# Moving a one-row sum to another engine and giving a batch the cheaper channel product, in a Fourier mixing kernel on one core

## The chip, the cores and the metric

The kernel runs on one core of a Trainium2 chip. A core has five engines with a queue each: TensorE (PE; its weight loads are listed as PEld), VectorE (DVE), ScalarE (ACT), GpSimd (POOL) and SyncE (SP), the last of which here only issues DMAs. The engines run side by side, each takes its instructions in order, and they wait for one another through semaphores. The metric is the device time of one execution in microseconds. Before the change it is 447.11 us, the median of three runs (446.85 to 447.27).

## The reference

```python
# x: [8, 3136, 256]   U: [3136, 32]   V: [32, 3136]   w_ch1: [256, 1024]   w_ch2: [1024, 256]
X = np.fft.fft(x, axis=1)                  # along the sequence
X = np.fft.fft(X, axis=2)                  # along the channels
x = X.real
xt = x.transpose(0, 2, 1)
h = xt @ U @ V                             # low-rank mixing along the sequence, rank 32
u = x + h.transpose(0, 2, 1)
ch = np.maximum(u @ w_ch1, 0.0) @ w_ch2    # two-layer product per token
out = u + ch
```

The real part of the two transforms is a product with cosines on both sides minus a product with sines on both sides.

## The kernel before, in words

**Stages.** The eight batches of 3136 rows are one list of 25088 output rows, worked in 49 chunks of 512 (`CH`). For a chunk `c` the main loop runs eight steps `j`. In each, `first_product(c, j)` multiplies the chunk's `u` with an eighth of `w_ch1` (two matmuls of 512 columns, L735) and ScalarE applies the relu on the way out of PSUM (L737). At every odd `j`, `second_product(c - 1, j // 2)` makes 128 rows of the chunk before (eight matmuls of 256 columns, L751); each second time VectorE adds `u` to it (L757 to L760) and so frees one of two PSUM buffers. At `j == 3`, `front(c + 1)` makes the next chunk's `u`: `low_product` (L709) multiplies the low-rank factors `TA` and `VA`, and VectorE adds the transformed input `S` or `T` to both halves (L725).

**A batch's transform** runs ahead of the chunks that need it, in steps hung between those of the main loop. `fold(b)` loads the batch in halves and takes sums and differences of mirrored channels (`along_d`, L386), of mirrored rows (`mirror`, L395) and of the two halves (`half`, L399), all on VectorE, into `G`. It also issues the next batch's loads on GpSimd's queue. `seq(b, par, typ, pn)` is the transform along the sequence on TensorE: `typ` 1 is the cosine (result `A`), 0 the sine (result `B`), `par` the parity of the output index, `pn` the parity of the input tile. The even tiles (`pn == 0`) are multiplied first and ScalarE keeps the result in `ev` (L489); after the odd tiles VectorE writes their sum into one half of `A` or `B` (L500) and their difference into the other (L504). A group of 425 columns holds 393 of the transform and 32 (`QW - NQ`) that carry `U` along, from which `TF`, and by `join_t` (L468) `TAB`, arise. `halves` (L430) and `quarters` (L446) are cheaper forms of an even group: matmuls over about half of the columns, from which VectorE makes the other half with a sum and a difference (L436, L437). Before, batches from `B0 = 2` on use `quarters`; the second batch (`b == 1`) uses `halves` for the cosine alone; the first batch uses neither.

**The channel product** turns `A` and `B` into `S` and `T`. In the batches from `B0` on, `even_ch` (one matmul from `A`, L643; ScalarE keeps it, L645) and `odd_ch` (one matmul from `B`, L652) give `S` and `T` as their sum and difference on VectorE (L654), and `across` copies rows of `A` into the lower 64 rows of `VA` on ScalarE (L664, L666). The first two batches use `chan` instead: for each of four pieces and each half one matmul from `A` and one from `B` into the same PSUM buffer (L631, L633), which ScalarE copies out (L635); and `last_row` (L684) fills a row of `VA` on VectorE.

**The narrow part.** The channel with index 0 has a column of its own in `G`. `narrow` transforms it in 16 matmuls with a stationary operand 32 wide (L556); the result has one used row, at PSUM partitions 0, 32, 64 and 96 for the four combinations of parities. Six sums of one row follow: two of 32 elements (L570), two upward ones (L573) and two downward ones (L574). They go into `TF` and into row 32 (`R`) of `VA`, which `low_product` reads. For the first batch VectorE makes them straight from PSUM, and the downward ones later (`late`); for the second, GpSimd makes them from SBUF, after ScalarE has copied both halves out. For the six batches from `B0` on, one joint narrow part (`column_steps`) does it for all at once.

**What sets the order.** Up to the end of chunk 0's steps the order is the program's own (`manual_schedule`). From chunk 1 on a planner places the instructions, and those of `fold` keep their program order (`pin`). The steps between the main loop's are entered in `due` under the number 8 * c + j, by `spread(steps, lo, hi)`, which distributes a list evenly. Tiles of the setup phase lie in the pool `gen`, which is closed before the pool `cp` opens in the same space; the first tile of `cp` is `u0`, the first chunk's `u`, written in two halves at L977.

## Time and profile before

| | |
|---|---|
| Median of three runs | 447.11 us (446.85 to 447.27) |
| The profiled execution's own time | 447.31 us |
| Its span in the profile | 445.2 us |
| Granted TensorE clock | 1.00 of full speed |
| TensorE busy | 435.7 us, 98% |
| VectorE busy | 353.1 us, 79% |
| ScalarE busy | 297.5 us, 67% |
| GpSimd busy | 85.7 us, 19% |

A row of a timeline gives the start and the duration in microseconds, the engine, the line, the operation, the tiles (out <- in), partitions and elements, and how many such instructions were merged. In brackets stands idle time before it and what ended that. The durations of matmuls overlap, since the array is a pipeline: the distance from one start to the next is what a matmul takes of TensorE's time. A row of a group gives the count, the busy time and the mean of one in ns. A row of windows gives, for a stretch, the busy time and count of PE, PEld, DVE, ACT and POOL, then the granted clock, the DMA share and GB/s.

### The profile page before, as it was taken

What the parts mean: (1) busy time and instruction counts of PE and PEld (TensorE: products, weight loads), DVE (VectorE), ACT (ScalarE), POOL (GpSimd) and SP (SyncE); (2) the same over time, 40 slices, a digit from 0 to 9 for tenths busy, and PEclk for the clock granted to TensorE, in tenths of its full rate; (3) what the DMA queues carried; (4) which work ended last, traced back from release to release, by engine and by line L of the source; (5) the groups of instructions that cost most, each with busy time, mean ns of one, the idle gap of its engine ahead of it and who ended that gap; (6) DMA issues with size and microseconds to landing.
All of it is one profiled execution on the core that took longest, in us unless ns stands there. A gap on an engine that the chain in (4) does not pass through costs nothing.

```text
span 445.2 us, 8087 instructions
## 1 busy us (share of the span) xinstructions
PE 435.7 (98%) x2960; PEld 316.4 (71%) x3012; DVE 353.1 (79%) x838; ACT 297.5 (67%) x564; POOL 85.7 (19%) x144
## 2 busy tenths in 40 slices
PE   8999999999999999999999999999999999999997
PEld 6456766776677777777777777777777777777775
DVE  8879998888998799878998789878998776443433
ACT  8857747565885669655875569655876569656562
POOL 8973217300931002300211001300000000000000
PEclk9999999999999999999999999999999999999999
DMA  7998997995199437674779537782333332434343
GB/s 133 210 230 180 229 173 117 245 153 103 49 230 265 120 106 216 190 171 73 157 203 222 108 103 216 196 167 71 95 119 95 91 100 73 117 97 121 93 125 112
DMA packets 103249, 65.36 MB, mean 147 GB/s; under 512 B 73806, under 2 KB 99624, under 8 KB 100464
## 3 DMA queue, kind: packets, MB, share of 16 engines
q1 hardware_dynamic: 97528, 39.10, 40.1%
q0 software_dynamic: 5664, 25.75, 21.6%
q8 instruction: 23, 0.38, 0.3%
q14 instruction: 16, 0.13, 0.1%
q10 hardware_dynamic: 18, 0.00, 0.0%
HBM read 29.33 MB, written 25.69 MB: 124 GB/s over the span
## 4 chain that ended last, share of the span: by engine, by line
PE 91%; DVE 2%; DMA 2%; issue 1%; POOL 1%; ACT 1%; DVEq 0%; POOLq 0%
PE p L751 38%; PE p L735 35%; PE pt L485 6%; PE ph L709 5%; DMA xb<-in_x_dram,xidx 2%; PE ptq L446 2%; PE pst L643 1%; PE pst L652 1%; PE m L850 1%; PE ptc L556 1%; ACT h L737 0%; DVE eor L386 0%; PE pst L631 0%; DVE eof L386 0%; PE pst L633 0%
## 5 line engine op out<-in xcount | busy, mean ns | idle before, releaser
L737 ACT ACTIVATE h<-p 128x512 bf16<-128x512 f32 x392 | 222.0, 597 | 119.5 <-PE p L735 107.3
L735 PE MATMUL p<-u,w 128*128 128x512 bf16 x735 | 209.3, 379 | 1.2 <-DVE B L500 0.2
L751 PE MATMUL p<-w,h 128*128 128x256 bf16 x1568 | 203.0, 273 | 1.4
L751 PEld LDWEIGHTS <-h 128*128 128x128 bf16 x1568 | 153.2, 98 | 50.4 <-DVE o L760 0.3
L735 PEld LDWEIGHTS <-w 128*128 128x128 bf16 x784 | 106.1, 144 | 35.1 <-issue 2.0
L757 DVE TENSOR_TENSOR o<-p,ut 128x4 f32<-128x4 f32 (+1 forms) x100 | 16.2, 162 | 54.9 <-PE p L751 53.3
L759 DVE TENSOR_TENSOR o<-p,ut 128x254 f32<-128x254 f32 (+1 forms) x100 | 40.5, 405 | 0.0
L760 DVE TENSOR_TENSOR o<-p,ut 128x254 f32<-128x254 f32 (+1 forms) x100 | 40.5, 405 | 0.0
L468 POOL TENSOR_TENSOR tab<-tf 128x64 bf16<-128x64 f32 x7 | 3.1, 440 | 179.2 <-DVE tf L492 179.1
L386 DVE TENSOR_TENSOR eof<-xf 99x1024 bf16<-99x1024 f32 x28 | 35.8, 1293 | 0.0
L386 DVE TENSOR_TENSOR eor<-xr 99x1024 bf16<-99x1024 f32 x28 | 34.8, 1247 | 0.0
L725 DVE TENSOR_TENSOR u<-ph,S 128x512 bf16<-128x512 f32 (+23 forms) x63 | 34.3, 553 | 0.0
L725 DVE TENSOR_TENSOR u<-ph,T 128x512 bf16<-128x512 f32 (+23 forms) x63 | 34.2, 553 | 0.0
L55 POOL DMA_INDIRECT xf<-in_x_dram,xidx x14 | 17.3, 1234 | 62.0 <-DVE eof L386 48.5
L709 PE MATMUL ph<-va,ta 128*128 128x512 bf16 (+15 forms) x124 | 28.6, 328 | 0.3
L485 PEld LDWEIGHTS <-g 98*128 98x128 bf16 (+1 forms) x152 | 14.7, 98 | 13.1 <-issue 0.7
L395 DVE TENSOR_TENSOR eos<-eof,eor 99x1024 bf16<-99x1024 bf16 (+1 forms) x28 | 19.2, 702 | 0.0
L654 DVE TENSOR_TENSOR S<-evd,pst 128x392 bf16<-128x392 f32 (+1 forms) x24 | 13.5, 564 | 6.4 <-PE pst L652 4.1
L485 PE MATMUL pt<-tabs,g 98*128 98x425 bf16 x80 | 17.6, 344 | 0.0
L457 DVE TENSOR_TENSOR ev<-ptq,ex 128x131 f32<-128x131 f32 (+1 forms) x24 | 6.9, 289 | 12.9 <-ACT ex L450 12.9
L399 DVE TENSOR_TENSOR g<-eos 99x2048 bf16<-99x2048 bf16 (+1 forms) x14 | 16.9, 1217 | 0.0
L485 PE MATMUL pt<-tabc,g 98*128 98x425 bf16 x72 | 15.5, 344 | 0.0
(198 smaller groups left out, 381.0 us busy)
## 6 DMA issues: line engine op xcount, KB each, us to landing
out_dram<-o SPq DMA_DIRECT2D x48, 512.0 KB
xr<-in_x_dram POOLq DMA_DIRECT2D x14, 784.0 KB, 8.2
xb<-in_x_dram POOLq DMA_DIRECT2D x2, 392.0 KB, 7.9
ut<-u SPq DMA_TRANSPOSE x49
w<-in_moe_w_ch_dram POOLq DMA_DIRECT2D x1, 512.0 KB
out_dram<-o SPq DMA_DIRECT2D x4, 128.0 KB
va<-in_moe_V_dram POOLq DMA_DIRECT2D x2, 196.0 KB
w<-in_moe_w_ch_dram POOLq DMA_DIRECT2D x1, 256.0 KB, 7.2
```

The costliest lines, as they stand in the source:

```text
L55: nc.gpsimd.indirect_dma_start(out_, None, bass.AP(t.tensor, t.offset, [[w, rows], [1, w]]), bass.IndirectOffsetOnAxis(idx, 0), element_of ...
L386: pin(nc.vector.tensor_tensor(dst[:, a, :, part * P:(part + 1) * P].rearrange("p i (k t) -> p i k t", k=2), lo, hi, op=AL.subtract if part ...
L395: pin(nc.vector.tensor_tensor(EOS[:, a, :, cols], EOF_[:, a, :, cols], EOR_[:, a, ::-1][:, :, cols], op=op))
L399: pin(nc.vector.tensor_tensor(G[b % 2][par][:, :, cols], EOS[:, 0, :, cols], EOS[:, 1, :, cols], op=AL.add if par == 0 else AL.subtract))
L485: nc.tensor.matmul(pt[:], g[:kp(i), i, P * typ:P * (typ + 1)], tabs[typ][:kp(i), i, par, :], start=(n == 0), stop=(n == NI // 2 - 1))
L709: nc.tensor.matmul(ph, TA[b % 2][:k, s * P:(s + 1) * P], VA[b % 2][:k, lo:hi], start=start, stop=True)
L725: nc.vector.tensor_tensor(u[:, s, col:col + hi - lo], ph[:, col:col + hi - lo], src, op=AL.add)
L735: nc.tensor.matmul(p1[:], W1[:, s, j::JT], k["u"][:, s, :], start=(s == 0), stop=(s == 1))
L737: LAST[0] = nc.scalar.activation(k["h"][:, j, :], p1[:], AF.Relu)
L751: nc.tensor.matmul(p2[:, t % w, :], h[:, j, rs], W2[:, j, :], start=(j == 0), stop=(j == JT - 1))
L759: nc.vector.tensor_tensor(o[:, ts, 1:P], p2[:, :w, 1:P], ut[:, ts, 1:P], op=AL.add)
L760: nc.vector.tensor_tensor(o[:, ts, P + 1:D], p2[:, :w, P + 1:D], ut[:, tT, P - 1:0:-1], op=AL.add)
```

## The change

- **First batch, narrow part** (`single=True`): ScalarE copies the four used rows out of PSUM one by one, to partition 0 of two tiles in the pool `gen` (`parted`: two before the sums of the first parity, two in front of those of the second). GpSimd makes all six sums from them, the downward ones right behind the others. VectorE makes none. The tiles use the buffers of `pho`, which become wider.
- **Second batch, order**: its narrow part comes first in `transform`, ahead of the sequence transform. Its sums of 32 elements go to tiles of their own (`tc1`, `tr1`), which `joined` copies into `TAB`.
- **Second batch, sine**: its even sine groups use `halves` too.
- **Second batch, channels**: `even_ch`, `odd_ch` and `across` replace `chan`, `low_product` takes all 128 rows of `TA` and `VA`, and `last_row` is no longer called for it; fewer rows of its `VA` are zeroed.
- **Places in the order**: the second batch's fold and transform start two places earlier (2 and 21 instead of 4 and 23); the third batch's fold begins four places later and ends two later, its transform begins two later and ends where it did; six of the seven steps of the joint narrow part come two to three places later, and the last one a place earlier.

```diff
-        if pn == 0 and (b >= B0 or b == 1 and typ == 1):
+        if pn == 0 and b:
             (quarters if b >= B0 else halves)(d, g, par, typ)
...
+    tc1 = cpool.tile([1, 2, R], FP32, name="tc1")
+    tr1 = cpool.tile([1, R], BF16, name="tr1")
...
-    def narrow(nb, stationary, dst, tc_, total, tag=("dft", 3), late=None, eng=None):
+    def narrow(nb, stationary, dst, tc_, total, tag=("dft", 3), single=False):
...
-        eng = eng or nc.vector
+        eng = nc.gpsimd
+        late = []
...
+            if single:
+                parted(0)
+                return
             t["ev"] = wp.tile([P, QW], FP32, tag="ev", name="evc", bufs=4)
             nc.scalar.copy(t["ev"][2 * R:], t["pt"][:2 * R])
-            if eng is nc.gpsimd:
-                t["pt"] = wp.tile([P, QW], FP32, tag="ev", name="evo", bufs=4)
-                nc.scalar.copy(t["pt"][2 * R:], pt[2 * R:])
+            t["pt"] = wp.tile([P, QW], FP32, tag="ev", name="evo", bufs=4)
+            nc.scalar.copy(t["pt"][2 * R:], pt[2 * R:])
+
+        def parted(par):
+
+            t[par] = gen.tile([KP, 2, QW], FP32, tag="pho", name="eo")[:1]
+            for pn in range(2):
+                g = (2 * pn + par) * R
+                nc.scalar.copy(t[par][:, pn], t["pt"][g:g + 1])
...
         def sums(par):
-            e, o = (t[k][(2 + par) * R:(2 + par) * R + nb] for k in ("ev", "pt"))
+            if single:
+                if par:
+                    parted(1)
+                e, o = t[par][:, 0], t[par][:, 1]
+            else:
+                e, o = (t[k][(2 + par) * R:(2 + par) * R + nb] for k in ("ev", "pt"))
...
-            if late is None:
-                down()
-            else:
-                late.append(down)
+            late.append(down)
+            if par or not single:
+                while late:
+                    late.pop(0)()
...
-        yield from narrow(1, lambda par, i: G[b][par][:kp(i), i, 256:256 + R], dst, TF[:1, 0],
-                          None, **kw)
+        yield from narrow(1, lambda par, i: G[b][par][:kp(i), i, 256:256 + R], dst,
+                          tc1 if b else TF[:1, 0], tr1[:] if b else None, **kw)
...
+        nc.gpsimd.tensor_copy(TS[:1, 0], trow[:, (b - B0) * R:(b - B0 + 1) * R] if b >= B0
+                              else tr1[:])
         if b >= B0:
-            nc.gpsimd.tensor_copy(TS[:1, 0], trow[:, (b - B0) * R:(b - B0 + 1) * R])
...
-        k = P if b >= B0 else 2 * R + 1
+        k = P if b else 2 * R + 1
...
     def transform(b):
 
+        if b < B0:
+            yield from first_channel(b)
         for par in range(2):
             for typ in (1, 0):
                 for pn in range(2):
                     yield lambda par=par, typ=typ, pn=pn: seq(b, par, typ, pn)
-        if b < B0:
-            row = list(first_channel(b, eng=nc.gpsimd))
-            yield from row[:2]
-            yield lambda: (row[2](), joined(b))
-            for ch in range(4):
-                for h in range(2):
-                    yield lambda ch=ch, h=h: chan(b, ch * 392 + (1 if ch else 0),
-                                                  (ch + 1) * 392 + 1, h)
-            yield from row[3:]
-            yield lambda: (lowrank(b), last_row(b))
-            return
         for ch in range(4):
             yield lambda ch=ch: (even_ch(b, ch), across(b, ch, False))
...
-        pho = gen.tile([KP, 2, NQ], I32, tag="pho", name="pho")
+        pho = gen.tile([KP, 2, QW], I32, tag="pho", name="pho")[:, :, :NQ]
...
-    narrow_0 = list(first_channel(0, tag=("p2", 2), late=late))
+    narrow_0 = list(first_channel(0, tag=("p2", 2), single=True))
...
-    for step in piece(1, 0) + piece(1, 1, tag=("p2", 2)) + late[2:] + late[:2]:
+    for step in piece(1, 0) + piece(1, 1, tag=("p2", 2)) + late:
...
-    va_zeros(1)
+    nc.gpsimd.memset(VA[1][R:2 * R].bitcast(I32), 0)
...
-            spread(list(fold(b)), 4, 23)
-            spread(list(transform(b)), 23, hi)
+            spread(list(fold(b)), 2, 21)
+            spread(list(transform(b)), 21, hi)
         else:
-            spread(list(fold(b)), hi - 66, hi - 35)
-            spread(list(transform(b)), hi - 33, hi)
+            lag = 2 if b == B0 else 0
+            spread(list(fold(b)), hi - 66 + 2 * lag, hi - 35 + lag)
+            spread(list(transform(b)), hi - 33 + lag, hi)
         if b == B0:
-            for at, step in zip((24, 23, 21, 20, 19, 18, 12), column_steps()):
+            for at, step in zip((21, 20, 18, 17, 16, 15, 13), column_steps()):
```

More of the change, by code (lines that the diff above doesn't have):

```diff
@@ L606, in column_steps @@
         yield from narrow(NB, lambda par, i: GC[par][:kp(i), i * NB:i * NB + R], rows, tc_,
-                          tcb[:], eng=nc.gpsimd)
+                          tcb[:])
         def finish():
@@ L775, in transform @@
                     yield lambda par=par, typ=typ, pn=pn: seq(b, par, typ, pn)
[L776 to L786 removed]
         for ch in range(4):
             yield lambda ch=ch: (even_ch(b, ch), across(b, ch, False))
[L789 removed]
+            yield lambda ch=ch: (odd_ch(b, ch), across(b, ch, True),
+                                 ch < 3 or joined(b))
         yield lambda: lowrank(b)
@@ L798, in odd_row @@
     def odd_row(i):
-        pho = gen.tile([KP, 2, NQ], I32, tag="pho", name="pho")
-        phase(pho[:], krow[:KP], ncol[:KP, i:i + 1], 15)
-        sine(tabs[0][:, i, :, :NQ], pho[:], 15, 1)
+        pho = gen.tile([KP, 2, QW], I32, tag="pho", name="pho")[:, :, :NQ]
+        phase(pho, krow[:KP], ncol[:KP, i:i + 1], 15)
+        sine(tabs[0][:, i, :, :NQ], pho, 15, 1)
     odd_row(0)
```

1 line of the change is left out of this document (removed).

## The prediction

> **What bounds the kernel now.** I read the page first (busy times, the chain that ended last), then the timeline of the stretches that the change touches: the start of the first batch (25 to 36 us) and the second batch's transform (50 to 85 us).
>
> ```profile
> span 445.2 us, 8087 instructions
> PE 435.7 (98%) x2960; PEld 316.4 (71%) x3012; DVE 353.1 (79%) x838; ACT 297.5 (67%) x564; POOL 85.7 (19%) x144
> PE 91%; DVE 2%; DMA 2%; issue 1%; POOL 1%; ACT 1%; DVEq 0%; POOLq 0%
> ```
>
> TensorE is busy for 98% of the span and makes 91% of the chain that ended last. So a matmul column less is time less, wherever TensorE does not wait; and every other engine counts only where it makes TensorE wait. The profiled execution took 447.31 us, 0.20 above the median of 447.11; the sum below is made against 447.31 and then lowered by that 0.20. A measurement of this kernel can tell about 0.2%, 0.9 us, from no change.
>
> **Matmuls removed.** The second batch's eight channel tiles are two matmuls each before (L631 and L633, 16 in all); after, four even and four odd products of the same width, 8 in all. Two of its four even-tile groups, the sine ones, become four matmuls of 229 columns in place of four of 425.
>
> ```profile
> 54.62 0.56 PE L430 MATMUL pth<-tabc,g 98*128 98x229 bf16 x4
> 55.02 0.88 PE L485 MATMUL pt<-tabc,g 98*128 98x425 bf16 x4
> 55.74 0.89 PE L485 MATMUL pt<-tabs,g 98*128 98x425 bf16 x4
> 68.15 0.33 PE L631 MATMUL pst<-A,mc 128*128 128x393 bf16 x1
> 68.32 0.33 PE L633 MATMUL pst<-B,msn 128*128 128x393 bf16 x1
> ```
>
> What counts is the distance of starts, since the durations overlap. Four of 229 columns take 55.02 - 54.62 = 0.40, four of 425 take 55.74 - 55.02 = 0.72: 2 x 0.32 = 0.64 less. A channel matmul takes 68.32 - 68.15 = 0.17, or 0.164 at the rate of the row of 425 (0.72 / 1700 columns): 8 x 0.164 = 1.31 less. Together **-1.95**. The narrow part is the same 16 matmuls, only earlier: 0.
>
> **The first batch's start.** Before, VectorE makes the six one-row sums straight from PSUM. After, ScalarE makes four copies of one row, and GpSimd the six sums, behind its product with `mc` (L951).
>
> ```profile
> 25.33 0.87 POOL L951 TENSOR_SCALAR mc<-mc 1x256 bf16<-1x256 bf16 x1
> 25.58 0.51 ACT L560 COPY evc<-ptc 64x425 f32<-64x425 f32 x1 [0.48 <-PE ptc L556]
> 30.07 0.59 PE L709 MATMUL pu<-va,ta 65*128 65x512 bf16 x2
> 30.53 0.58 ACT L977 CAST u<-pu 128x512 bf16<-128x512 f32 x1 [0.59 <-PE pu L709]
> 30.70 0.69 DVE L977 CAST u<-pu 128x512 bf16<-128x512 f32 x1 [1.11 <-PE pu L709]
> 31.17 1.52 PE L735 MATMUL p<-u,w 128*128 128x512 bf16 x6
> 31.31 0.44 DVE L635 CAST T<-pst 128x273 bf16<-128x273 f32 x1
> 31.66 1.06 DVE L504 TENSOR_TENSOR A<-ev,pt 128x392 bf16<-128x392 f32 x2
> 32.75 1.22 DVE L574 TENSOR_TENSOR va<-evc,ptc 1x392 bf16<-1x392 f32 x2
> 34.46 2.36 PE L735 MATMUL p<-u,w 128*128 128x512 bf16 x10
> 34.69 0.69 DVE L725 TENSOR_TENSOR u<-ph,S 128x512 bf16<-128x512 f32 x1
> 35.30 0.68 DVE L725 TENSOR_TENSOR u<-ph,T 128x512 bf16<-128x512 f32 x1
> 35.90 2.35 DVE L386 TENSOR_TENSOR eor<-xr 99x1024 bf16<-99x1024 f32 x2
> ```
>
> The second batch's own narrow sums on GpSimd, the same six of one row, are the price:
>
> ```profile
> 68.91 0.49 POOL L570 TENSOR_TENSOR tf<-evo,evc 1x32 f32<-1x32 f32 x1 [5.41 <-ACT evo L563]
> 69.46 1.02 POOL L573 TENSOR_TENSOR va<-evo,evc 1x393 bf16<-1x393 f32 x1
> 70.44 1.47 POOL L574 TENSOR_TENSOR va<-evc,evo 1x392 bf16<-1x392 f32 x1
> 71.97 0.25 POOL L570 TENSOR_TENSOR tf<-evo,evc 1x32 f32<-1x32 f32 x1
> 72.28 1.38 POOL L573 TENSOR_TENSOR va<-evo,evc 1x392 bf16<-1x392 f32 x1
> 73.62 1.02 POOL L574 TENSOR_TENSOR va<-evc,evo 1x392 bf16<-1x392 f32 x1
> ```
>
> GpSimd is free of L951 at 25.33 + 0.87 = 26.20. The first two copies, at 0.51 each from 25.58, end at 26.60, so the sums start there. Uncontended they take 0.49 + 0.25 + 4 x 1.02 = 4.82, with starts about 0.05 apart some 5.05: they end at 31.65. What waits for that decides. The rows for `u0` (L709, at 30.07) need only the two upward sums, done near 29.5: in time. But the copies lie in the setup pool `gen`, and `u0` is the first tile in `cp`, which takes over that space: in the built program both copies that write `u0` wait for the last of the six sums. They start at 31.65 instead of 30.53, and the first product moves from 31.17 to 32.3: **+1.1**. TensorE has nothing else to do there. Ends: with the four long sums at 1.0 and the short ones at 0.25 they take 4.5 and end at 31.1, +0.55; with the rows' own sum of 5.63 and the gaps they end near 32.5, +1.9. I take the middle, because the stretched rows (1.47, 1.38) ran beside VectorE work from SBUF, and here VectorE works from PSUM. The four copies instead of one delay ScalarE's copy of the next even group by half a copy; VectorE, freed of the four upward sums, still waits for TensorE's last group of the batch, so nothing is gained there. If that cover fails, the loss lies within the upper end.
>
> What is next late: the second chunk's `u`. VectorE, from 31.65, has in its queue after: `u0` 0.61 (30.70 to 31.31), T 0.35 (to 31.66), the two A parts 1.09 (to 32.75), a fold sum (L386) 2.35 / 2 = 1.18, a T copy of 392 columns 0.50 (0.35 x 392 / 273), another fold sum 1.18, and only then the two `u` sums. The fold, two places earlier, has put 2.35 ahead of them, and the 1.22 of downward sums has gone. They start at 31.65 + 4.9 = 36.55 and end at 36.55 + 0.61 + 0.68 = 37.85. TensorE wants the second at 34.46 + 9 x 0.215 + 1.1 = 37.5: **+0.4** (0 to 0.9; more only if the first step's end is late, which is counted there).
>
> **Third chunk to sixth.** The chunk that begins at 52.73 waits for VectorE already:
>
> ```profile
> 51.67 1.04 PE L751 MATMUL p<-w,h 128*128 128x256 bf16 x8
> 52.73 0.65 PE L735 MATMUL p<-u,w 128*128 128x512 bf16 x2
> 53.24 2.37 DVE L399 TENSOR_TENSOR g<-eos 99x2064 bf16<-99x2064 bf16 x2
> ```
>
> Eight at 0.107 would end at 52.53: 0.2 of waiting. After, the two `g` sums (2.37) stand ahead of that chunk's `u`, and the narrow products, 0.7 of TensorE work brought forward, ahead of that chunk too. Before, that `u` was done when the `g` sums began, at 53.24. VectorE's queue up to there is now longer by 2.37 - 1.22 = 1.15 and starts 0.95 later (31.65 against 30.70): `u` is done at 55.3, its first half 0.6 sooner. TensorE, not held up, comes there at 52.53 + 1.5 + 0.7 = 54.7, or 54.9 with narrow products that no longer run side by side, and wants the second half one product later, at 55.1. The two meet, and most of the old 0.2 is swallowed by the new shift: **-0.1** (-0.2 to +0.6).
>
> From there to the chunk whose first product is at 84.60, the added VectorE work is the four-by-two sums of the channel product and two pairs of sums of the sine halves; the last-row sum goes.
>
> ```profile
> L654 DVE TENSOR_TENSOR S<-evd,pst 128x392 bf16<-128x392 f32 x18 | 10.1, 563 | 4.0 <-ACT h L737 2.0 <-PE pst L652 1.8
> 56.26 0.35 DVE L436 TENSOR_TENSOR ev<-pth,ev 128x196 f32<-128x196 f32 x1
> 56.65 0.40 DVE L437 TENSOR_TENSOR ev<-pth,ev 128x229 f32<-128x229 f32 x1
> 76.57 0.97 DVE L684 TENSOR_TENSOR va<-S,T 1x1567 bf16<-1x1567 bf16 x1 [0.85 <-ACT T L635]
> 69.88 1.15 DVE L395 TENSOR_TENSOR eos<-eof,eor 99x1024 bf16<-99x1024 bf16 x1
> 72.04 0.73 DVE L395 TENSOR_TENSOR eos<-eof,eor 99x1024 bf16<-99x1024 bf16 x1
> 73.89 1.82 DVE L386 TENSOR_TENSOR eof<-xf 99x1024 bf16<-99x1024 f32 x1
> 78.29 1.81 DVE L386 TENSOR_TENSOR eof<-xf 99x1024 bf16<-99x1024 f32 x1
> sum 35.00, PE 34.52 PEld 24.03 DVE 32.77 ACT 21.38 POOL 16.29; mean PE 4.93 PEld 3.43 DVE 4.68 ACT 3.05 POOL 2.33
> 84.60 0.81 PE L735 MATMUL p<-u,w 128*128 128x512 bf16 x3
> ```
>
> The sum row is of 50 to 85 us. Added: 8 x 0.563 + 2 x 0.75 = 6.0; gone: 0.97, and (1.15 - 0.73) + (1.82 - 1.18) + (1.81 - 1.18) = 1.7, since GpSimd's narrow sums, beside which those three were stretched, now run while VectorE takes sums out of PSUM; and two fold sums (2.35) of the third batch, which is delayed by four places, fall behind 85. So 32.8 + 6.0 - 5.0 = 33.8 of demand in 35 - 1.95 + 1.3 = 34.4. VectorE is just full, and its order decides. Following the new queue, I find TensorE waiting about 0.5 for the B half before an odd product, 0.2 at one `u` and 0.4 at the next, 1.1; some 0.9 of such waits go, of which 35.00 - 34.52 = 0.5 shows as idle and the rest, an estimate, lies under the overlapping durations. **+0.2** (-0.6 to +1.8). ScalarE's eight added row copies of 64 partitions replace eight channel copies, and it has 13 us free of 35: 0, and under 0.5 if a relu slipped behind one.
>
> **After the sixth chunk** the same work is done in the same order with the third batch's transform in two places fewer and the column sums on GpSimd about three places later. Both still fall beside the fourth batch's fold, as before: 0 (-0.5 to +0.7).
>
> **Sum.** -1.95 + 1.1 + 0.4 - 0.1 + 0.2 = -0.35: 447.31 - 0.35 = 446.96, on the median's level 446.76, say **446.7**.
>
> **Rivals.**
> *Nothing is paid at the start.* If GpSimd's one-row sums at partition 0 are quick enough to end by 30.5, the first product and the second chunk stand still, and 1.5 of the sum goes: 447.11 - 1.95 - 0.1 + 0.2 = 445.3, faster. It needs six sums in 3.9 us instead of 5.05; against it stand all six rows, none of the long ones below 1.02. The same outcome comes if VectorE's relief (1.7 of stretched sums) removes waits that I still count, or if the first batch's late start is made up before 85 us because VectorE, not TensorE, set the pace in the old windows. Chance 0.27. The Trainium skill (GPSIMD Engine Reference, section 3.1) gives about 2.6 cycles an element at 1.2 GHz for a sum of two inputs; from that, as an estimate, a sum of 392 elements takes 0.85 us and the six 3.5, which would end them at 30.1 and give this rival's time. The row of 1.02 is longer than the Trainium skill's 0.85, so by the trace the rule sets too low a price here.
> *VectorE becomes the bound in the second batch.* Its place is the chunk of 84.60: if the queue reaches that `u` later than TensorE, every us goes into the span. Demand of 33.8 stands against 34.4; the first us of excess decides, for instance two of its fold sums stretched to 1.8 again, or sums queued behind an even copy that is late. Two us over, with 0.6 of slack, and the late start at its upper end give -0.35 + 1.4 + 0.8 = +1.85: 449.0, slower. For it: VectorE's 32.77 of 35. Against it: the delayed fold leaves work that can slip past 85, where the next windows have room. Chance 0.22.
> *The change moves nothing that can be told.* This is my forecast, or the case in which its two large terms (-1.95 and +1.5) miss by a like amount. Chance of the forecast 0.51.
>
> **How the numbers follow.** The forecast's own range is 445.9 to 447.6; the part of it below 446.2 holds 0.13. So faster 0.27 + 0.13 = 0.40, slower 0.22, same 0.38. The range takes in most of both rivals: 444.9 to 448.8; I leave about 0.1 on either side of it.
>
> **What would show it.** Right: GpSimd's sixth sum ends near 31.6 and both copies into `u0` start just behind it; the first product of w1 is at about 32.3; the second chunk's first products are split by a short wait for VectorE; the L386 rows of the third batch are back at 1.2; the chunk that was at 84.60 begins at about 84.5 with a part of the next second product already done. Wrong: `u0` copied before 31, or the sixth sum after 32.5; windows between 60 and 95 in which TensorE is busy under 4.8 of 5 with VectorE as the releaser; a shift that arises only after 90 us.

## The result, and the profile after

The changed kernel takes 454.67 us (median of 6 runs, 452.35 to 455.48) against 447.10 for the kernel before, six runs beside it. By the medians it is slower by 7.6 us, and far outside the predicted range; the ratio of the mean times is 1.016, 95% interval 1.0136 to 1.0184. Ratios here and below are of means, so they can differ a little from those of the medians. One execution of all those below, of e10 (453.1 us at a granted clock of 0.992), was in a slow state, and its ratio leaves it out. The profiled execution of the changed kernel took 454.9 us. Lines of the changed kernel have other numbers than before: L727 is `low_product` (L709 before), L743 the `u` sums (L725), L753 and L769 the two products (L735, L751), L587 to L591 the narrow sums (L570 to L574), L627 the copy of the joint rows (L610).

From the page of the kernel after: span, busy times, the granted clock by 40 slices, and the chain that ended last.

```profile
span 453.1 us, 8152 instructions
PE 439.9 (97%) x3004; PEld 316.9 (70%) x3004; DVE 353.3 (78%) x843; ACT 301.3 (66%) x571; POOL 83.7 (18%) x151
PEclk9999999999997999999999999999999999999999
PE 88%; DMA 4%; DVE 2%; ACT 2%; POOL 2%; issue 1%; DVEq 0%; POOLq 0%; SPq 0%; ACTq 0%
```

No engine's share of the span rose. One slice, the 13th (136 to 147 us), has a lower clock, and DMA's share of the chain doubled. The view of what TensorE waited for names the place at once (three of its lines):

```profile
PE ph L727 <- DMA va<-rows: 4.5, 1, 4.5
PE ph L727 <- ACT evd L662: 0.9, 1, 0.9
PE ptt L696 <- DVE tab L468: 0.8, 1, 0.8
```

To see where each microsecond went, I took for every chunk the start of its first relu (the rows of L737 before, L755 after) and subtracted the time before. For the changed kernel the differences are +0.52 at chunk 0, +0.89 at chunk 1, +1.97 at chunk 3, +0.14 at chunk 8, +0.10 at chunk 10, +0.97 at chunk 11, **+7.43 at chunk 12**, and from there to the last chunk between 7.43 and 7.53. Nearly all of the loss, 6.5, arises from chunk 11 to chunk 12, the one that holds the border of the second and the third batch.

**What happens there.** Timeline of the kernel after:

```profile
116.25 1.03 POOL L55 DMA_INDIRECT xf<-in_x_dram,xidx  x1 [3.57 <-DVE eof L386]
122.12 0.24 POOL L587 TENSOR_TENSOR tc<-evo,evc 6x32 f32<-6x32 f32 x1 [4.84 <-DMA xf<-in_x_dram,xidx]
127.93 1.48 POOL L627 COPY rows<-rows 6x1567 bf16<-6x1567 bf16 x1
129.69 0.63 SPq L691 DMA_DIRECT2D va<-rows  x1
133.23 0.22 PE L727 MATMUL ph<-va,ta 128*128 128x128 bf16 x1
137.93 0.91 PE L727 MATMUL ph<-va,ta 128*128 128x384 bf16 x3 [4.49 <-DMA va<-rows]
```

And of the kernel before:

```profile
112.02 0.24 POOL L570 TENSOR_TENSOR tc<-evo,evc 6x32 f32<-6x32 f32 x1 [1.34 <-issue]
121.24 0.62 SPq L673 DMA_DIRECT2D va<-rows  x1
122.56 1.02 POOL L55 DMA_INDIRECT xf<-in_x_dram,xidx  x1 [0.20 <-DVE eor L386]
132.64 0.61 PE L709 MATMUL ph<-va,ta 65*128 65x128 bf16 x4
```

Before, GpSimd makes the joint narrow sums at 112, copies the rows, and only then issues the gather that loads the first half of the fifth batch. After, the joint steps are later in the order, and that gather stands ahead of the sums in GpSimd's queue. The first sum then waits until the gather has landed (122.12, 5.87 after its issue), the sums end at 127.4 and the copy at 129.4, and the DMA that brings the third batch's row into `VA` is issued at 129.69 in place of 121.24. TensorE wants that row at 133.4 and gets it at 137.93. The built programs say the same of the wait. A semaphore is a counter, which here a landed load raises by 16; these are the values ahead of the first joint sum:

```
after:  gather xf raises DMASW6 from 48 to 64;  then  wait DMASW6 >= 64;  sum tc
before: sum tc (waits DMASW2 >= 64, an older gather);  ...  gather xf raises DMASW6 to 64
```

**And the clock.** Windows of the kernel after: stretch, sum of stretch, busy time and count of PE, PEld, DVE, ACT, POOL, then the granted clock.

```profile
134.00:136.00 2.00, 0.00 (x0) 0.00 (x0) 2.00 (x5) 0.00 (x0) 1.91 (x2) 0.91 1.76 231
138.00:140.00 2.00, 2.00 (x7) 0.89 (x7) 1.42 (x4) 0.27 (x1) 0.00 (x0) 0.50 1.05 388
142.00:144.00 2.00, 2.00 (x15) 1.36 (x13) 0.00 (x0) 1.09 (x2) 0.00 (x0) 0.89 0.89 306
```

The clock falls to half while TensorE stands still and is back at full only after 142: the first products behind the wait run at half speed. (Windows of 1 us have 0.81 from 135 to 136 and 0.78 from 142 to 143, which puts the fall near 135.6 and the return near 142.4.) It is no accident of the profiled execution: the mean granted clock was 0.992 to 0.996 in all six. The Trainium skill (TensorE: Matmul & The Clock Gate, "Why this matters for your kernels") warns of idle gaps of more than about 3 us between matmuls, after which the array is back at half rate; the gap of 4.49 agrees.

**The start**, where I had looked hardest, went nearly as forecast. Timeline of the kernel after:

```profile
28.40 1.00 POOL L590 TENSOR_TENSOR va<-eo 1x392 bf16<-1x392 f32 x1
29.37 1.70 POOL L591 TENSOR_TENSOR va<-eo 1x392 bf16<-1x392 f32 x2
31.11 0.58 ACT L987 CAST u<-pu 128x512 bf16<-128x512 f32 x1 [0.77 <-POOL va L591]
31.15 0.69 DVE L987 CAST u<-pu 128x512 bf16<-128x512 f32 x1 [1.17 <-POOL va L591]
31.75 1.46 PE L753 MATMUL p<-u,w 128*128 128x512 bf16 x6 [0.21 <-ACT u L987]
36.90 0.44 PE L753 MATMUL p<-u,w 128*128 128x512 bf16 x1 [0.23 <-DVE u L743]
37.50 0.38 PE L753 MATMUL p<-u,w 128*128 128x512 bf16 x1 [0.15 <-DVE u L743]
```

GpSimd ends at 31.07 (forecast 31.65), both copies into `u0` wait for its last sum, the first product starts at 31.75, and the second chunk's first products are split by two short waits for VectorE.

**The second batch's channel product** holds two waits that I had not forecast. (L681 copies backward rows, L683 forward ones.) Timeline of the kernel after:

```profile
72.57 0.52 ACT L681 COPY va<-A 64x392 bf16<-64x392 bf16 x1
73.11 0.48 ACT L662 COPY evd<-pst 128x392 f32<-128x392 f32 x1
73.65 0.38 PE L727 MATMUL ph<-va,ta 65*128 65x512 bf16 x1 [0.94 <-ACT evd L662]
77.79 0.33 PE L660 MATMUL pst<-A,me 128*128 128x392 bf16 x1 [0.45 <-ACT evd L662]
```

Row copies into `VA` (L681, L683) stand in ScalarE's queue ahead of the copies that free PSUM (L662), and TensorE waits for these.

### The profile page after: what moved, and what is told of

Same layout as the page of the kernel before. It is cut to its first block, busy times and chain, and to the rows that moved or that the text cites. A ratio compares the mean times of both kernels' runs of the same rounds, so it can differ in the third digit from the quotient of the medians.

```text
span 453.1 us, 8152 instructions
## 1 busy us (share of the span) xinstructions
PE 439.9 (97%) x3004; PEld 316.9 (70%) x3004; DVE 353.3 (78%) x843; ACT 301.3 (66%) x571; POOL 83.7 (18%) x151
## 4 chain that ended last, share of the span: by engine, by line
PE 88%; DMA 4%; DVE 2%; ACT 2%; POOL 2%; issue 1%; DVEq 0%; POOLq 0%; SPq 0%; ACTq 0%
PE p L769 36%; PE p L753 36%; PE pt L485 5%; PE ph L727 4%; DMA xb<-in_x_dram,xidx 2%; DMA va<-rows 2%; PE ptq L446 2%; PE pst L660 1%; PE pst L669 1%; PE m L860 1%; ACT h L755 1%; PE ptc L559 1%; DVE u L743 1%; DVE eor L386 1%; ACT eo L575 0%
## 5 line engine op out<-in xcount | busy, mean ns | idle before, releaser
L755 ACT ACTIVATE h<-p 128x512 bf16<-128x512 f32 x392 | 221.2, 597 | 125.5 <-PE p L753 122.6
L753 PE MATMUL p<-u,w 128*128 128x512 bf16 x784 | 218.9, 381 | 0.7 <-DVE u L743 0.4
L769 PE MATMUL p<-w,h 128*128 128x256 bf16 x1568 | 205.1, 273 | 0.0
L769 PEld LDWEIGHTS <-h 128*128 128x128 bf16 x1568 | 153.6, 98 | 53.0 <-issue 1.7
L753 PEld LDWEIGHTS <-w 128*128 128x128 bf16 x784 | 106.4, 144 | 36.4 <-issue 3.3
L743 DVE TENSOR_TENSOR u<-ph,T 128x512 bf16<-128x512 f32 (+23 forms) x63 | 34.3, 555 | 2.1 <-PE ph L727 2.1
L727 PE MATMUL ph<-va,ta 128*128 128x512 bf16 (+16 forms) x126 | 29.7, 332 | 5.4 <-DMA va<-rows 4.5
L743 DVE TENSOR_TENSOR u<-ph,S 128x512 bf16<-128x512 f32 (+23 forms) x63 | 34.4, 555 | 0.0
L386 DVE TENSOR_TENSOR eor<-xr 99x1024 bf16<-99x1024 f32 x28 | 34.0, 1216 | 0.0
L386 DVE TENSOR_TENSOR eof<-xf 99x1024 bf16<-99x1024 f32 x28 | 33.9, 1230 | 0.0
L671 DVE TENSOR_TENSOR S<-evd,pst 128x392 bf16<-128x392 f32 (+1 forms) x28 | 15.7, 562 | 7.2 <-PE pst L669 4.1
L727 PEld LDWEIGHTS <-ta 128*128 128x128 bf16 (+1 forms) x128 | 12.0, 98 | 7.5 <-issue 4.8
L485 PE MATMUL pt<-tabs,g 98*128 98x425 bf16 x72 | 15.8, 344 | 0.0
```

The costliest lines, as they stand in the source:

```text
L386: pin(nc.vector.tensor_tensor(dst[:, a, :, part * P:(part + 1) * P].rearrange("p i (k t) -> p i k t", k=2), lo, hi, op=AL.subtract if part ...
L485: nc.tensor.matmul(pt[:], g[:kp(i), i, P * typ:P * (typ + 1)], tabs[typ][:kp(i), i, par, :], start=(n == 0), stop=(n == NI // 2 - 1))
L727: nc.tensor.matmul(ph, TA[b % 2][:k, s * P:(s + 1) * P], VA[b % 2][:k, lo:hi], start=start, stop=True)
L743: nc.vector.tensor_tensor(u[:, s, col:col + hi - lo], ph[:, col:col + hi - lo], src, op=AL.add)
L753: nc.tensor.matmul(p1[:], W1[:, s, j::JT], k["u"][:, s, :], start=(s == 0), stop=(s == 1))
L755: LAST[0] = nc.scalar.activation(k["h"][:, j, :], p1[:], AF.Relu)
```

## The experiments

All times in one table first. The shifts are those of the first relu of a chunk against the kernel before, in the profiled execution. Kernels whose start is that of before begin chunk 0 between -0.35 and +0.13, so that much of any shift is the start's own drift. The kernels were timed in four groups, each beside the kernel before. Its medians were 447.17 (e1, e3, e4, e5), 447.08 (e6 to e9), 447.17 (e10 to e12) and 447.12 (e13).

| kernel | median us | ratio to before (95%) | chunk 0 | 1 | 3 | 8 | 12 |
|---|---|---|---|---|---|---|---|
| after | 454.67 | 1.0160 (1.0136 to 1.0184) | +0.52 | +0.89 | +1.97 | +0.14 | +7.43 |
| e1 joint steps back | 448.53 | 1.0029 (1.0017 to 1.0040) | +0.61 | +0.99 | +2.07 | +0.25 | +1.24 |
| e3 before, joint steps late | 447.16 | 1.0006 (0.9996 to 1.0017) | +0.07 | +0.07 | +0.05 | +0.07 | -0.20 |
| e4 TensorE kept busy | 453.91 | 1.0153 (1.0133 to 1.0174) | +0.62 | +1.01 | +2.09 | +0.26 | +5.69 |
| e5 gather later | 447.28 | 1.0001 (0.9991 to 1.0011) | +0.73 | +1.12 | +2.20 | +0.39 | +0.34 |
| e6 before, third batch's places | 448.83 | 1.0045 (1.0026 to 1.0065) | -0.35 | -0.35 | -0.36 | -1.52 | +1.56 |
| e7 e5, row copies later | 445.81 | 0.9973 (0.9962 to 0.9983) | +0.72 | +1.10 | +2.17 | -1.17 | -1.21 |
| e8 e5, first sums on VectorE | 447.93 | 1.0018 (1.0008 to 1.0028) | -0.25 | +1.36 | +2.43 | +0.61 | +0.56 |
| e9 e7 and e8 | 446.43 | 0.9993 (0.9983 to 1.0002) | +0.13 | +1.74 | +2.81 | -0.16 | -0.20 |
| e10 e6, gather later | 445.99 | 0.9974 (0.9964 to 0.9983) | -0.13 | -0.13 | -0.13 | -1.29 | -1.32 |
| e11 e7, old fold places | 446.23 | 0.9976 (0.9966 to 0.9986) | +0.84 | +0.64 | +0.65 | -0.49 | -0.54 |
| e12 e9, old fold places | 445.99 | 0.9973 (0.9964 to 0.9983) | -0.09 | -0.08 | -0.09 | -1.60 | -1.64 |
| e13 e12, fewer row copies | 445.51 | 0.9958 (0.9942 to 0.9975) | +0.13 | +0.13 | +0.12 | -1.87 | -1.92 |

**e1: the joint steps at their old places.** From after:

```diff
-            for at, step in zip((21, 20, 18, 17, 16, 15, 13), column_steps()):
+            for at, step in zip((24, 23, 21, 20, 19, 18, 12), column_steps()):
```

> The changed kernel with the seven steps of the joint narrow part at their old places (24, 23, 21, 20, 19, 18, 12 before the end); all else as changed. Theory Q (queue): the 6.5 us that are lost at the thirteenth chunk arise because the joint sums on GpSimd stand behind the gather for the fifth batch and wait for its landing; in this build the gather stands behind the sums and behind the copy of the rows. So the wait of TensorE for the DMA into VA (4.5 us) and the stretch at half clock after it go: 446.6 to 447.6 us, no difference from before that can be told, with the shift at the thirteenth chunk between 0 and +1. Rival V (VectorE): the second batch's added VectorE work is what is lost and shows only there: 453 us or more, as before this edit.

Measured 448.53, above the range that I gave. (Six of the seven steps come three places later in the change, not two to three.) The sums start at 112.99, the gather comes at 122.68 behind the rows' copy, no half clock, and the shift at chunk 12 is +1.24: 6.1 us of the loss go with one line of places. That it stays 1.25 above e5 (below) isn't explained. In the profiled executions e1 is 0.14 ahead of e5 at chunk 8 and 0.9 behind it at chunk 12, and another 0.4 lies behind the first relu of the last chunk (13.74 to the end of the span, against 13.37).

**e3: the same places in the kernel before**, the change of e1 the other way round and nothing else.

> The kernel before with only the seven places of the joint narrow part changed as in the change (21, 20, 18, 17, 16, 15, 13). In this build the gather for the fifth batch stands between the last sum and the copy of the rows. Theory Q: the sums wait for no gather; the copy of the rows may start 2 to 3 us later than before, which the slack of the row (issued at 121.2, wanted at 133) covers: 446.5 to 448 us. Rival L: the later places alone cost most of the 7.5 us: 451 to 454 us.

Measured 447.16, no change. The sums start at 116.00, four microseconds later than before, and TensorE waits for no row; the gather comes at 123.16, still behind them. Late places alone cost nothing; the order against the gather does.

**e5: only the gather held back.** From after: the load of the fifth batch's first half is issued behind the last joint sum, everything else stays.

```diff
-                yield lambda a=a: load_half(b + 1, a)
+                yield lambda a=a: load_behind(b + 1, a)
...
+    def load_behind(b, a):
+        if (b, a) != (4, 0):
+            load_half(b, a)
+            return
+        with tc.issue_after(DOWN[0].ins):
+            load_half(b, a)
...
+            def down():
+                DOWN[0] = eng.tensor_tensor(dn, e[:, 1:NQ], o[:, 1:NQ], op=AL.subtract)
```

> The changed kernel, every place as changed, but the gather for the first half of the fifth batch is held until the last of the joint sums has been issued. Theory Q: the sums start when ScalarE's copies are there, near 116.6 instead of 122.1; the DMA into VA goes out near 124 to 126 and lands before TensorE wants the row at 133: 447 to 448.5 us. Rival L (late places): the sums are late because their places are later, not because of the gather; then the row still arrives after 136 and the time stays at 452 or more.

Measured 447.28, a ratio of 1.0001. Timeline of e5 (L597 is the sum, L638 the rows' copy):

```profile
116.35 0.24 POOL L597 TENSOR_TENSOR tc<-evo,evc 6x32 f32<-6x32 f32 x1 [3.42 <-ACT evo L578]
123.47 1.04 POOL L55 DMA_INDIRECT xf<-in_x_dram,xidx  x1 [0.32 <-POOL rows L602]
124.56 1.48 POOL L638 COPY rows<-rows 6x1567 bf16<-6x1567 bf16 x1
```

The sums start as late as in e3, the gather 7.2 us later than in after, and TensorE waits for no row. 454.67 - 447.28 = 7.4 us is the price of the gather's place (7.1 by the ratios), and what is left, a ratio of 1.0001, is no loss that can be told. Two more things are seen here. In the built program of e5 the sum's wait is for 48 of that semaphore, an older transfer. And the rows' copy, right behind the gather, starts 1.09 after it: GpSimd does not stand still behind a gather as such. It was the wait that the program gives to the first joint sum. Why the program waits there for a transfer whose tile the sum doesn't read is open.

**e4: TensorE kept busy in the wait.** From after, with 44 matmuls of 256 columns, whose result is not used, ahead of chunk 12's `low_product`: the wait stays, the clock does not fall.

```diff
+    due.setdefault(8 * 11 + 3, []).append(lambda: busy(44))
```

> The changed kernel with 44 matmuls of ones by ones (128x256, into an unused PSUM tile) put in front of the low-rank product of the thirteenth chunk; they add work that no result uses. They fill some 4.7 us, in the time in which TensorE waits for the row. Theory C (clock): about 2.5 of the 7.5 us lost are the stretch at half clock after the wait, so with TensorE kept busy the granted clock stays at 1.00 there and the time falls to about 452 us, with the wait for the row still to be seen in its start. Rival: the wait alone makes the loss, or the clock falls all the same: 454.5 us or more.

Measured 453.91 (two runs), between the two forecasts. Timeline of e4:

```profile
133.49 4.97 PE L175 MATMUL idle<-ones 128*128 128x256 bf16 x44
138.29 0.64 PE L727 MATMUL ph<-va,ta 128*128 128x128 bf16 x4
```

The clock is 1.000 throughout, `low_product` comes 0.36 later than in after, and yet chunk 12 begins 1.74 earlier (+5.69 against +7.43), and stays 1.75 ahead to the last chunk. From the end of the wait to that relu after takes 6.75 (137.93 to 144.68) and e4 4.65 (138.29 to 142.94): 2.1 us of the shift are the half clock, the other 5.3 the wait and what stood before it. That fits the windows above: some 4.5 us of matmuls at half clock (137.93 to 142.4) cost, as an estimate, half of that. The whole times differ by only 0.8, which two runs can't tell from the spread of after (452.35 to 455.48). In the profiled runs the tail behind the last chunk's first relu was 1.0 longer in e4 (14.7 against 13.7), all of it behind VectorE's last sum; why is open. So the price of the clock is read from one execution of each kernel, not from the times.

**e6: the third batch's new places in the kernel before.** Fold four places later, transform two later, and the joint steps as in the change; the second batch as before.

```diff
-            spread(list(fold(b)), hi - 66, hi - 35)
-            spread(list(transform(b)), hi - 33, hi)
+            lag = 2 if b == B0 else 0
+            spread(list(fold(b)), hi - 66 + 2 * lag, hi - 35 + lag)
+            spread(list(transform(b)), hi - 33 + lag, hi)
...
-            for at, step in zip((24, 23, 21, 20, 19, 18, 12), column_steps()):
+            for at, step in zip((21, 20, 18, 17, 16, 15, 13), column_steps()):
```

> The kernel before with only the two edits of places: the third batch's fold and transform later (lag 2) and the seven steps of the joint narrow part at 21, 20, 18, 17, 16, 15, 13. With both, the built program has the gather for the fifth batch ahead of the joint sums on GpSimd, as the changed kernel has; with the steps alone it had not. Theory Q: this gives the whole loss without any of the change's other parts: the joint sums start near 122, TensorE waits some 4 us for the row at the thirteenth chunk, granted clock down after it, 452 to 456 us. Rival: the loss needs the second batch's new work too, and the time is 446.5 to 448.5 us.

Measured 448.83: the mechanism came, the size was missed. Timeline of e6, and one window (columns as above):

```profile
114.59 1.01 POOL L55 DMA_INDIRECT xf<-in_x_dram,xidx  x1 [3.63 <-DVE eof L386]
120.46 0.24 POOL L570 TENSOR_TENSOR tc<-evo,evc 6x32 f32<-6x32 f32 x1 [4.86 <-DMA xf<-in_x_dram,xidx]
127.80 0.62 SPq L673 DMA_DIRECT2D va<-rows  x1
134.26 0.55 PE L709 MATMUL ph<-va,ta 128*128 128x384 bf16 x3 [2.47 <-DMA va<-rows]
132.00:134.00 2.00, 0.00 (x0) 0.00 (x0) 2.00 (x5) 0.00 (x0) 2.00 (x2) 1.00 0.98 242
```

The same wait of the sum for the gather (5.87 from issue to start, as in after), but the row's DMA was issued at 127.80 and awaited until 134.26, 6.5 us, where in after it took 8.2. TensorE stood still for 2.47, and the clock did not fall in this execution. Two of the eight, the longest (450.44 and 450.89), had a mean granted clock of 0.996, the others 0.999 or 1.000; so there it may have fallen. Places alone flip the order, and it takes both edits: with the new joint steps alone (e3), or with the third batch's new places and the old joint steps (e1), the gather stayed behind the sums. It also shows a gain that I had not looked for, -1.5 at chunk 8.

**e10: e6 with the gather held back** as in e5. (The text on record names the second batch's places too; the kernel, like e6, leaves them as before.)

> The kernel before with the new places alone (second and third batch's fold and transform, joint narrow part), as in e6, and in addition the gather of the fifth batch's first half held until the last joint sum. The 'gather' theory: the joint sums start about 116 again, no wait for the row's DMA, and what the places gained by chunk 9 in e6 (1.2 to 1.6 us once its earlier start of 0.35 is taken off) stays: 445.4 to 446.2. The rival, that the later third transform needs the gather early or the gain was only work moved past chunk 9: the gain is gone by chunk 12, 446.8 to 447.4.

Measured 445.99, a ratio of 0.9974: 1.2 us faster than before, with nothing changed but places in the order and the held gather. The gain stays to the end (-1.32 at chunk 12). Where it comes from, before:

```profile
58.21 1.21 DVE L386 TENSOR_TENSOR eof<-xf 99x1024 bf16<-99x1024 f32 x1
60.40 1.22 DVE L386 TENSOR_TENSOR eof<-xf 99x1024 bf16<-99x1024 f32 x1
66.83 0.91 PE L556 MATMUL ptc<-tabc,g 98*32 98x425 bf16 x16
```

and in e10:

```profile
62.80 1.22 DVE L386 TENSOR_TENSOR eof<-xf 99x1024 bf16<-99x1024 f32 x1
65.03 1.19 DVE L386 TENSOR_TENSOR eof<-xf 99x1024 bf16<-99x1024 f32 x1
63.76 0.91 PE L566 MATMUL ptc<-tabc,g 98*32 98x425 bf16 x16
```

Two fold sums of the third batch stood among VectorE's sums of the second batch's transform; in e10 they come after most of these, and the narrow products, last of that transform, start at 63.76 instead of 66.83. Not all of these 3 us is time gained, since other work stood in between; the medians say 1.2. The third batch's transform was moved too, and its part was not tried apart.

**e7: ScalarE's row copies out of the way.** From e5: the second batch's four backward row copies (`across(b, ch, True)`) go behind its channel product, to the steps 45, 48, 51 and 54, where chunks that need them are still ahead.

```diff
-            yield lambda ch=ch: (odd_ch(b, ch), across(b, ch, True),
+            yield lambda ch=ch: (odd_ch(b, ch), b == 1 or across(b, ch, True),
...
+    for ch in range(4):
+        due.setdefault(45 + 3 * ch, []).append(lambda ch=ch: across(1, ch, True))
```

> The changed kernel with the gather held behind the joint sums (as in the run with 447.28 us), and the second batch's four backward row copies on ScalarE taken out of its channel product and put into later steps (from chunk 5 on). Theory S (ScalarE): in that channel product TensorE waits 0.94 and 0.45 us for copies of even products that stand behind row copies on ScalarE, 1.1 and 0.6 us of stall between starts; they go, and the time falls by 1.0 to 1.7 us to 445.6 to 446.3. Rival: those waits only take the place of waits for VectorE in the same chunks, and the time stays within 0.4 of 447.3.

Measured 445.81, 1.5 under e5 (1.3 by the ratios): both waits for the copies of even products (L662 in after) are gone, and chunk 8 begins at -1.17 instead of +0.39. The copies that I had costed at 0 cost 1.5 where they stood.

**e8 and e9: the first part of the change undone.** From e5 and from e7: the first batch's narrow sums go to VectorE straight from PSUM, as before; the downward ones late in its queue, as before.

```diff
-        eng = nc.gpsimd
-        late = []
+        eng = nc.vector if single else nc.gpsimd
+        late = LATE if single else []
...
-    for step in piece(1, 0) + piece(1, 1, tag=("p2", 2)) + late:
+    for step in piece(1, 0) + piece(1, 1, tag=("p2", 2)) + late + LATE:
```

> The changed kernel with the gather held behind the joint sums, and the first batch's narrow sums back on VectorE from PSUM, the downward ones last, as before. Theory of the prediction: the first part of the change costs the start of the main loop 0.5 us and the second chunk another 0.4 to 0.6, together 0.9 to 1.2, and nothing later wins it back: 446.1 to 446.5 us. Rival: the later chunks wait for VectorE anyway, so its relief was worth the late start: 447.2 us or more.

> Both of these together: row copies later and the first batch's sums back on VectorE, gather held behind the joint sums. If the two losses are in different places and add, 444.4 to 445.4 us, faster than before by 0.4% or more; if they share a cover, not below 445.8.

Measured 447.93 and 446.43, 0.65 and 0.62 slower than with GpSimd. Neither theory came: e8 came out at its rival's time, and in e9 the two gains did not add. Chunk 0 begins 0.6 to 1.0 earlier, but by chunk 1 another 1.61 is lost, where e5 and e7 lose 0.39 and 0.38. Timeline of e9 (L599 a downward sum, L751 `u`):

```profile
32.89 1.22 DVE L599 TENSOR_TENSOR va<-evc,ptc 1x392 bf16<-1x392 f32 x2
34.14 1.23 DVE L386 TENSOR_TENSOR eor<-xr 99x1024 bf16<-99x1024 f32 x1
35.88 1.22 DVE L386 TENSOR_TENSOR eor<-xr 99x1024 bf16<-99x1024 f32 x1
37.02 0.68 DVE L751 TENSOR_TENSOR u<-ph,S 128x512 bf16<-128x512 f32 x1
37.75 0.44 PE L761 MATMUL p<-u,w 128*128 128x512 bf16 x1 [1.27 <-DVE u L751]
```

With the fold's two sums ahead of the second chunk's `u`, the downward sums on VectorE are what is too much.

**e11 and e12: the second batch's fold and transform at their old places**, from e7 and e9.

```diff
-            spread(list(fold(b)), 2, 21)
-            spread(list(transform(b)), 21, hi)
+            spread(list(fold(b)), 4, 23)
+            spread(list(transform(b)), 23, hi)
```

> e7 (gather held, the second batch's four backward row copies later) with the second batch's fold and transform at the old places (4 to 23, 23 on). Theory that the earlier fold delays the second chunk's u: chunk 1 begins 0.3 to 0.4 earlier against chunk 0 than in e7 (the split of 0.35 there goes), and the time is 445.2 to 445.6. Rival, that what is saved at chunk 1 is paid at the third or fourth chunk, where the second batch's transform is due: 445.8 to 446.6.

> e9 (as e7, with the first batch's narrow sums on VectorE as before) with the second batch's fold and transform at the old places. In e9 VectorE's sums cost 0.62 us against GpSimd's, because two fold sums and the downward sums stood ahead of the second chunk's u. Theory that this was the earlier fold: chunk 1 begins within 0.3 of the kernel before, and the time is equal to or under that of e11: 444.6 to 445.4. Rival, that GpSimd's sums are worth it whatever the fold does: 0.4 to 0.8 above e11.

Measured 446.23 and 445.99. In both, the wait at chunk 1 goes: against chunk 0 it begins 0.20 earlier in e11 (0.38 later in e7) and at 0.01 in e12 (1.61 later in e9). In e12 VectorE takes the `u` at 34.61 and the fold's sums behind it. But in e11 more is lost later, as the rival had it: in the profiled executions -0.54 at chunk 12 against -1.21 in e7, and 446.23 against 445.81 in the medians, though the two intervals do not tell these apart. For e12 the gain stays, 0.44 in the medians, although its time is above the range that I gave. So what GpSimd's sums are worth depends on the fold's place: with the fold early they gain 0.6, with the old places they are 0.24 the slower, which the two intervals do not tell from nothing.

**e13: fewer row copies on ScalarE, once more.** e12 against e10 had no gain in the medians (445.99 both), with 1.95 us of matmuls fewer. Timeline of e12 (L691 a forward row copy, L670 the copy out of PSUM):

```profile
72.23 0.52 ACT L691 COPY va<-A 64x392 bf16<-64x392 bf16 x1
72.78 0.49 ACT L670 COPY evd<-pst 128x392 f32<-128x392 f32 x1
73.31 0.38 PE L735 MATMUL ph<-va,ta 65*128 65x512 bf16 x1 [0.70 <-ACT evd L670]
```

So two of the four forward copies go later too:

```diff
-            yield lambda ch=ch: (even_ch(b, ch), across(b, ch, False))
+            yield lambda ch=ch: (even_ch(b, ch),
+                                 b == 1 and ch > 1 or across(b, ch, False))
...
+    for ch in (2, 3):
+        due.setdefault(40 + 2 * ch, []).append(lambda ch=ch: across(1, ch, False))
```

> e12 with two of the second batch's four forward row copies on ScalarE moved behind its channel product too (to the steps 44 and 46). e12 takes as long as e10, though it has 1.95 us of matmuls fewer; in e12 TensorE still waits 0.70 for the second even copy of the channel product, ahead of which the third forward row copy (0.52) stands. ScalarE theory: that wait shrinks to under 0.3 and the time falls by 0.4 to 0.7 us, 445.3 to 445.6. Rival, that VectorE is the one that is full there (5.00 busy of 5 in the windows from 65 to 75): the wait only moves to VectorE's sums or to a u, and the time is that of e12, 445.8 to 446.2.

Measured 445.51, a ratio of 0.9958 (0.9942 to 0.9975), the lowest median of all kernels here and faster than the kernel before. TensorE's second `low_product` there waits for nothing:

```profile
72.84 0.38 PE L735 MATMUL ph<-va,ta 65*128 65x512 bf16 x1
```

That wait was ScalarE's, then. Counted from chunk 0, e13 is 0.5 ahead of e12 by chunk 12, as the medians have it, though 0.5 lies within the intervals of e12 and e13. e13 is the change without its first part and without the second batch's earlier fold, and with the gather and six row copies put where nobody waits for them.

## Why the prediction was wrong

**The step that failed** is "After the sixth chunk", costed at 0 (-0.5 to +0.7). I wrote that the same work is done in the same order, with the column sums on GpSimd about three places later. The order was not the same: on GpSimd's queue the fifth batch's gather came to stand ahead of the joint sums (after, 116.25 and 122.12). I looked at what the moved steps stood beside on TensorE and VectorE, and did not write down GpSimd's new queue or follow the moved step to its end: sums, rows' copy, row DMA, `low_product`. Before, the row's DMA was issued 11.4 us ahead of its use (121.24 and 132.64). Its issue moved by 8.45 and its use by 0.8, which left 3.8 us (129.69 to 133.44) for a DMA that was awaited for 6.5 (e6) to 8.2 (after). What I had put at 0 cost 7.4 of the 7.6, as e5 shows: a wait of 4.49, some 2.1 of half clock behind it, and under 1 ahead of it. None of my rivals named it; the one that forecast a loss had VectorE for its mechanism.

**The part before it looked right for wrong reasons.** The sum up to the sixth chunk was -0.35, and chunks 8 to 10 came to between -0.28 and +0.14. But the terms did not, and that their sum did was luck:

- *Matmuls, -1.95*: not measured alone. e12 and e13 differ from e10 only in the second batch's transform, and are 0.0 and 0.5 faster in the medians; even with ScalarE out of the way, most of what TensorE saves is not seen in the time. ScalarE's waits were a part of that, which e13 shows; what holds the rest is open.
- *The first batch's start, +1.1 and +0.4*: the mechanism (GpSimd's last sum holds `u0` through the pool) is shown by what ended the waits. Sizes: +0.52 at chunk 0, since the downward sums took 0.85 each, the price that the first rival goes by, and not 1.02, so GpSimd ended at 31.07, my lower end; and +0.37 more at chunk 1, as forecast. What I had wrong is the comparison: with the fold two places earlier, leaving the sums on VectorE costs 0.6 more (e8, e9). Within this change the first part is a gain.
- *Third chunk, -0.1*: +0.92 from chunk 2 to chunk 3, of which 0.7 is the narrow products brought forward, as I had them. About 0.2 is a loss, within the range given.
- *VectorE "just full", +0.2*: VectorE ended none of TensorE's waits between 60 and 95 us. The relief was real: the L386 sums of the third batch are back at 1.2, and the delay of its fold and transform, of which I entered only the fold, as 2.35 of demand, was worth 1.2 by itself (e10 against e3, which have the joint steps alike). The waits I followed in its queue did not come.
- *ScalarE, 0*: the mis-sized term. I gave it "13 us free of 35" and "under 0.5 if a relu slipped behind one". Not a relu but the copy that frees a PSUM buffer slipped behind the row copies, twice: 1.5 (e7 against e5). An average over 35 us hid that 70 to 80 was nearly full. Windows of the kernel after (ScalarE is the fourth busy time, 4.59 and 4.44 of 5):

```profile
70.00:75.00 5.00, 4.06 (x28) 2.77 (x27) 5.00 (x12) 4.59 (x10) 1.61 (x4) 1.00 0.94 254
75.00:80.00 5.00, 4.55 (x31) 3.22 (x30) 4.25 (x10) 4.44 (x9) 0.00 (x0) 1.00 1.19 179
```

So -1.2 from the third batch's delay and +1.5 from ScalarE, both outside my sum, roughly cancelled. They were measured one at a time on different kernels, and no run shows that all the terms add up. The marker that I gave for the channel product, the chunk at 84.60 beginning at 84.5, was off by 2.2 (chunk 6's relu is at +2.16), because more of the other work came ahead of it; by chunk 8 that was made up. The marker that I gave for being wrong, "a shift that arises only after 90 us", is what came.

## What to carry to other kernels

When steps are moved in an order that a planner completes, write down the new queue of every engine around them, and of the DMAs it issues above all: three places' delay cost nothing by itself (e3), and 7.4 us when, together with the third batch's new places, it let a load slip ahead. Follow a moved step to whoever uses its last product, and compare the slack there with the time from issue to use that the same DMA needs in the trace. And do not cost copies on a half-idle engine at nothing before looking at the few microseconds in which they stand: a copy that frees a buffer for the busiest engine must not queue behind copies that nobody wants yet.

## What the hardware showed that I had not expected

- The granted clock fell to 0.50 in an idle gap of 4.49 us and stayed there for some 4.5 us of matmuls behind it, which cost about 2.1 us on top of the wait (after against e4). A gap of 2.47 us left it at 1.00 (e6). The two profiled gaps lie on either side of the 3 us in the Trainium skill, cited above, and agree with it; but in after the clock fell some 2.2 us into the gap (133.45 to about 135.6), and the mean clock of 0.996 in two other executions of e6 leaves open whether shorter gaps are safe.
- The same small DMA of one row, `va<-rows`, took from its issue to the matmul that waited for it 6.5 us in e6 and 8.2 in after.
- One-row sums on GpSimd from partition 0 took 1.00 for an upward one and 0.85 for a downward one. The join of two tiles on VectorE, which before took 0.22, took 0.61 beside them:

```profile
28.87 0.22 DVE L468 TENSOR_TENSOR tab<-tf 128x64 bf16<-128x64 f32 x1
```

```profile
28.88 0.61 DVE L468 TENSOR_TENSOR tab<-tf 128x64 bf16<-128x64 f32 x1
```

The first is the timeline of before, the second of after, where GpSimd's upward sum (28.40 to 29.40) overlaps it; before, GpSimd only zeroed a tile there (28.21 to 29.61). TensorE waited 0.77 for it, under the cover of the wait for GpSimd. The Trainium skill (SBUF — State Buffer, "Who interferes with whom") says that a VectorE instruction with two inputs from SBUF and a GpSimd one that reads SBUF exclude each other on a shared port; the join ends 0.09 after the sum (29.49 and 29.40), which agrees.
